# An attention and two-expert-layer kernel: the unit sizes of its last stage, the times its weights are split, and the order of its loads

## The chip, the cores and the metric

One core of a Trainium2 chip runs the whole kernel. The metric is the device time of one execution in microseconds (us); the kernel before takes 880.95 us, the median of three runs.

## What is computed

Attention over 4 batches and 8 heads of 64, with 32 global and 512 local rows each; a dense two-layer network on all 2176 rows; then a second network in which each row goes to one of eight experts. Only the last part is changed:

```python
logits = xn @ en.T / tau
expert_idx = np.argmax(logits, axis=1)
...
gate_w = probs[np.arange(N), expert_idx]
for e in range(E):                      # E = 8
    mask = expert_idx == e
    h = np.maximum(x[mask] @ w1[e], 0.0)        # w1[e]: 512 x 1024
    out[mask] = gate_w[mask, None] * (h @ w2[e])  # w2[e]: 1024 x 512
```

All data are float32. With the inputs of this case, the reference sends 153, 561, 160, 57, 46, 102, 1028 and 69 rows to the experts 0 to 7.

## The kernel before

**Stages.** Attention (slices 0 to 7 of the profile, roughly) runs beside the first steps of the dense network, whose rest (`L1`, `L2`, lines 678 to 712) follows; the logits and gates of finished rows are made along the way (`R0` to `R3`, for the last 384 rows `Q0` to `Q4`). The normal end of it is the expert stage, from about 618 us on. Rows with their gate lie in a table in memory, `x2d`; lists of row numbers, sorted by expert, lie in `idl`, padded so that each list may be read over its end. `make_plan` works out on DVE (on one partition) which list and which expert each unit gets, and leaves this in the tile `plan`.

**Units.** The expert stage is a fixed row of units, whatever the routing is. A unit fetches rows with an indirect DMA on the POOL queue (`gather`, line 857), transposes them on PE (`X2`, lines 929 to 952; 128x128 pieces against an identity), and runs both products. There are three kinds:

- Dense units of 256 rows (`D1`, line 1048, and `D2`, line 1066): for each of eight blocks of 128 hidden columns `D1` makes h transposed with twelve matmuls, ACT makes the relu of it (line 1054), DVE the rest that ACT's rounding leaves (line 1055), and `D2`, one step later, adds six matmuls to two output tiles. To keep float32's accuracy at the fast rate, weights and rows are held as a rounded part and a rest, and three of the four products are done.
- Units of 128 rows (`M1`, `M2`): the same with rows on the output's partitions, in two halves of 512 hidden columns each, and h transposed back by PE (`HT`, line 986).
- Mixed units of two rests of up to 64 rows of two experts (`X1`, line 974, and `X2M`, line 1033). Each half of PE's columns takes its own rows, and so the two experts' matmuls stand in pairs, in plain float32 on raw weights. A pass is `X1` or `X2M` for one half of the hidden columns; a unit has four passes.

The order is `ORDER` = 0, 1, 2, 3, S, 4, S, 5, 6, 7, mixed, mixed: eight dense units, two of 128 (S) and two mixed. Units 0 to 2 are planned before the last 384 rows are routed (phase 0 of `make_plan`), the others in three more phases that stand as pieces in units 0 to 3. What is over after all of this would be done by the code behind (`rest`, lines 1345 to 1366), under two branches on counts, which all engines read at the end.

**Weights.** One expert's weights are two matrices of 2.1 MB. `load_w` (lines 851 to 855) has SP read the expert from `plan` and issue the two loads, into lane a (`w1a`, `w2a`) or lane b (`w1b`, `w2b`). Where a unit has the expert of the one before it, the condition makes the load a no-op, but its weights are split again: `piece` (with `split`, lines 867 to 874) is a rounding copy on ACT (line 870) and a subtraction on DVE (line 871), over a quarter of a matrix. Each unit that isn't mixed has eight pieces, so 80 in all, written by the functions `some` and `ready` between the steps of the unit before. Split halves and lane b live in eight buffers called "half" (2.1 MB each).

**What sets the order.** In the expert stage DVE, ACT, SP and PE run in the order in which the code is written (`manual_schedule`). The function `unit` (lines 1278 to 1321) writes the steps, `due` (line 1323) hangs other work on a step, and `pend` holds second products back by a step.

## Time and profile before

| | |
|---|---|
| three runs, median (lowest to highest) | 880.95 us (880.47 to 881.92) |
| the profiled execution: its own time | 878.23 us |
| its span in the trace | 876.5 us |
| mean granted clock of PE | 0.973 |
| PE busy | 827.3 us, 94% |
| DVE, ACT, POOL busy | 502.8, 458.3, 159.8 us (57%, 52%, 18%) |
| moved by DMA | 91.73 MB, mean 105 GB/s |
| chain that ended last | PE 74%, DVE 7%, DMA 7%, issue 6%, ACT 5% |

The span is what the trace covers of the profiled execution, and all places in time are counted from its start. PE is a matmul, PEld the weight load of one, DVE, ACT and POOL the vector, scalar and general engine, SP the engine that issues most DMAs; a q behind a name is the engine's queue of instructions that aren't counted as busy. The granted clock is a share of 2.4 GHz. The trace leaves buffer and some tensor numbers out, and so `in_moe_w_dram` is either weight tensor of the experts. It shows every float32 matmul of a mixed unit as two records.

### The profile page before, as it was taken

The numbers are of one execution on the slowest core, as the hardware profiler recorded it, in microseconds if no ns is written. First come the engines' busy times: TensorE is split into PE (matmuls) and PEld (weight loads), VectorE is DVE, ScalarE is ACT, GpSimd is POOL, SyncE is SP. The second block draws the span as 40 slices with busy tenths as digits, with TensorE's granted clock in tenths as the row PEclk, the third lists the DMA queues.
The fourth block names the chain that finished last, engine by engine and source line by source line (L and its number), as shares of the span: only waits on it lengthen the run. The fifth ranks groups of instructions, "written<-read, shape, count | busy, mean of one in ns | idle before, by whom it ended". The sixth has DMA issues, their size and how long they took to land.

```text
span 876.5 us, 15818 instructions
## 1 busy us (share of the span) xinstructions
PE 827.3 (94%) x5764; PEld 694.3 (79%) x5764; DVE 502.8 (57%) x1369; ACT 458.3 (52%) x1143; POOL 159.8 (18%) x212
## 2 busy tenths in 40 slices
PE   6676698999999999999999999999999999999996
PEld 3554587888888888888888889889898988889841
DVE  6878989534654555365454442456678666766200
ACT  6877888444454545454453322325555566665221
POOL 3533354100120010010000000002113232421000
PEclk8787899999999999999999999999999999999998
DMA  8686555011012122011000000043042977716950
GB/s 237 179 214 164 149 165 144 20 40 37 25 43 48 30 59 46 13 47 33 2 13 13 1 25 1 13 151 103 25 37 78 380 257 250 244 69 236 365 211 19
DMA packets 103980, 91.73 MB, mean 105 GB/s; under 512 B 72967, under 2 KB 81287, under 8 KB 103890
## 3 DMA queue, kind: packets, MB, share of 16 engines
q1 hardware_dynamic: 97746, 78.51, 30.0%
q0 software_dynamic: 3744, 9.72, 3.3%
q10 hardware_dynamic: 2400, 2.36, 0.9%
q8 instruction: 49, 0.80, 0.5%
q14 instruction: 41, 0.34, 0.2%
HBM read 97.03 MB, written 11.10 MB: 123 GB/s over the span
## 4 chain that ended last, share of the span: by engine, by line
PE 74%; DVE 7%; DMA 7%; issue 6%; ACT 5%; SPq 0%; POOL 0%; ACTq 0%; POOLq 0%; DVEq 0%
PE hps L688 21%; PE hps L1048 8%; PE yp L710 7%; PE yp L1066 7%; PE yp L712 7%; PE yp L711 7%; DMA out_dram<-yo,ids 3%; PE av L256 2%; PE pp L242 2%; PE sp L205 2%; PE ga L317 2%; ACT pr L226 2%; DVE pr L232 1%; PE yp L1015 1%; PE hp L961 1%
## 5 line engine op out<-in xcount | busy, mean ns | idle before, releaser
L695 ACT COPY gf<-hps 128x256 f32<-128x256 f32 (+1 forms) x144 | 50.3, 361 | 173.9 <-PE hps L688 173.1
L696 DVE SCALAR_TENSOR_TENSOR gf<-gf 128x256 f32<-128x256 f32 (+1 forms) x144 | 60.0, 426 | 131.7 <-ACT gf L695 131.3
L710 PE MATMUL yp<-woh,g 128*128 128x512 f32 x272 | 114.2, 420 | 0.8 <-ACT g L698 0.8
L712 PE MATMUL yp<-woh,g 128*128 128x512 f32 x272 | 107.7, 396 | 1.5 <-DVE g L699 1.5
L711 PE MATMUL yp<-wol,g 128*128 128x512 f32 x272 | 107.4, 395 | 0.0
L1066 PE MATMUL yp<-w2s,g 128*128 128x512 f32 x384 | 101.0, 395 | 0.1
L699 DVE TENSOR_TENSOR g<-gf,g 128x256 fp32r<-128x256 f32 (+1 forms) x144 | 60.9, 431 | 42.8 <-ACT g L698 37.7
L1048 PE MATMUL hps<-xgT,w1s 128*128 128x256 f32 x512 | 82.6, 283 | 0.9 <-ACT xgT L947 0.9
L1066 PEld LDWEIGHTS yp<-w2s,g 128*128 128x128 f32 x384 | 67.5, 187 | 14.1 <-issue 1.6
L688 PE MATMUL hps<-xs,wih 128*128 128x256 f32 x448 | 75.6, 291 | 2.7 <-ACT gf L695 2.7
L1048 PEld LDWEIGHTS hps<-xgT,w1s 128*128 128x128 f32 x512 | 72.2, 188 | 5.6 <-ACT xgT L947 1.3
L698 ACT CAST g<-gf 128x256 fp32r<-128x256 f32 (+1 forms) x144 | 55.3, 395 | 35.0 <-DVE gf L696 34.9
L688 PEld LDWEIGHTS hps<-xs,wih 128*128 128x128 f32 x448 | 65.1, 189 | 9.3 <-ACT gf L695 3.1
L688 PE MATMUL hps<-xs,wil 128*128 128x256 f32 x448 | 71.2, 280 | 0.0
L688 PE MATMUL hps<-xl,wih 128*128 128x256 f32 x448 | 71.1, 280 | 0.0
L1054 ACT ACTIVATE g<-hps 128x256 fp32r<-128x256 f32 x64 | 24.6, 384 | 74.9 <-PE hps L1048 72.6
L712 PEld LDWEIGHTS yp<-woh,g 128*128 128x128 f32 x272 | 51.0, 188 | 14.6 <-DVE g L699 2.4
L710 PEld LDWEIGHTS yp<-woh,g 128*128 128x128 f32 x272 | 51.1, 188 | 12.8 <-issue 4.1
L688 PEld LDWEIGHTS hps<-xs,wil 128*128 128x128 f32 x448 | 60.9, 189 | 0.0
L688 PEld LDWEIGHTS hps<-xl,wih 128*128 128x128 f32 x448 | 60.9, 189 | 0.0
L711 PEld LDWEIGHTS yp<-wol,g 128*128 128x128 f32 x272 | 51.3, 188 | 6.5
L242 PE MATMUL pp<-ident,pr 128*128 128x128 f32 x256 | 41.7, 291 | 7.8 <-DVE pr L232 4.2
(285 smaller groups left out, 1625.2 us busy)
## 6 DMA issues: line engine op xcount, KB each, us to landing
w1a<-in_moe_w_dram SPq DMA_DIRECT2D x8, 2048.0 KB
w2a<-in_moe_w_dram SPq DMA_DIRECT2D x8, 2048.0 KB
w1b<-in_moe_w_dram SPq DMA_DIRECT2D x4, 2048.0 KB
w2b<-in_moe_w_dram SPq DMA_DIRECT2D x4, 2048.0 KB
wm<-in_moe_w_dram SPq DMA_DIRECT2D x4, 2048.0 KB
raw<-in_moe_w_in_dram SPq DMA_DIRECT2D x14, 512.0 KB
raw<-in_moe_w_out_dram SPq DMA_DIRECT2D x14, 512.0 KB
x2d<-x SPq DMA_DIRECT2D x16, 256.5 KB
```

The source lines that it names most:

```text
L242: nc.tensor.transpose(pp[:, j, :], pr[:, j // 2, (j % 2) * P:(j % 2) * P + P], ident)
L688: nc.tensor.matmul(hps, ws[a][:, k], xs[c][k], start=(a + c + k == 0), stop=((a, c) == (1, 0) and k == KM - 1))
L695: nc.scalar.copy(gf, hps[:, cs])
L696: nc.vector.scalar_tensor_tensor(out=gf, in0=gf, scalar=0.01, in1=gf, op0=ALU.mult, op1=ALU.max)
L698: nc.scalar.copy(g[:, 0], gf)
L699: nc.vector.tensor_tensor(out=g[:, 1], in0=gf, in1=g[:, 0].bitcast(F32), op=ALU.subtract)
L710: nc.tensor.matmul(yp, g[:, 0], hi, start=(f == 0), stop=False)
L711: nc.tensor.matmul(yp, g[:, 0], lo, start=False, stop=False)
L712: nc.tensor.matmul(yp, g[:, 1], hi, start=False, stop=(f == KF - 1))
L1048: nc.tensor.matmul(hps, w[:, a, k, fs], xts[u][c][:, k], start=(a + c + k == 0), stop=(a == 1 and k == KM - 1))
L1054: nc.scalar.activation(out=g[:, 0], in_=hps, func=AF.Relu)
L1066: nc.tensor.matmul(ys[u, t], g[:, a, t * P:(t + 1) * P], w[:, c, f % 4, :], start=(f + a + c == 0), stop=(f == KF2 - 1 and a == 1),)
```

## The change

The stage gets another row of units (`FIRST`): 0, 1, 2, S0, 3, QU, NE, NE + 1, S1, X0, S2, XL. There are six dense units, three of 128 rows (S0, S1, S2), two mixed ones of two halves (X0, XL) and a new one, QU, of four rests of up to 32 rows.

- Units 0 to 3 are all of the expert with most rows, NE and NE + 1 (4 and 5) of the second. Their weights are loaded and split once each (`weights_of`, `used_up`); with the three units of 128 that makes 5 × 8 = 40 pieces.
- `X1` and `X2M` take a list of two or four weights; with four, each matmul has 32 columns of its own (`tile_position`). The first products of QU stand ahead of NE, the second ones behind NE's last steps (`hold=True`).
- `early_plan` finds the two experts and `late_plan` makes all lists of 128, 64 and 32 in one pass (`lists`; a rest over 96 rows goes to a list of 128, one over 32 to a list of 64, others to a list of 32), in five pieces in units 0 and 1.
- Loads stand at fixed places, in `due`: `s_load` for a unit of 128, `f_load` for the second expert, `part_load` for the raw matrices of the rests; these go into "half" buffers or into lane a. QU has 16.8 MB of weights, X0 and XL have 8.39 MB each. Thirteen experts are loaded where there were ten.
- One branch on the count of unplaced lists (`more`) is left of two; the plan for what is over (`left_plan`) is made only inside it.

The core of the diff; the plan's own arithmetic is left out:

```diff
-    NDE, ND, NS, NM = 3, 8, 2, 2
-    NX = NBLK - 2 * (ND - NDE)
-    NENT, NCOL = ND + NX + E, 2 * ND + NX + E
-    HENT = ND + NX
+    QUART = P // 4
+    NE, NF, NS, NM = 4, 2, 3, 2
+    NEARLY = NE - 1
...
+    ND = NE + NF
+    SU, XU, QU, LU = ND, ND + NS, ND + NS + NM, ND + NS + NM + 1
...
+    SIZES = (P, HALF, QUART)
+    FEWEST = (96, 32, 0)
...
-    ORDER = [0, 1, 2, 3, ND, 4, ND + 1, 5, 6, 7, MIX, MIX + 1]
-    LANES = [[0, 1, 2, 3, 4, 5, 6, HENT], [ND, ND + 1, 7, HENT + 1]]
...
+    def weights_of(u):
+        return 0 if u < NE else NE if u < ND else u
...
+    def load_w(col, into, cond=False):
+        e = nc.sync.value_load(plan[0:1, 1, col:col + 1], min_val=0, max_val=E - 1)
+        cond = dict(cond=nc.sync.value_load(plan[0:1, 2, col:col + 1], min_val=0, max_val=1)) if cond else {}
+        for w, src in into:
             nc.sync.dma_start(w, src[bass.ds(e, 1)].rearrange("o (k p) f -> p (o k) f", p=P), **cond)
...
+    def to_split(w, pair, late_second):
+        sources[w] = pair
         order = [(1, 0), (1, 1), (2, 0), (2, 1)] if late_second else [(1, 0), (2, 0), (1, 1), (2, 1)]
-        return [(u, m, j, i) for m, j in order for i in range(2)]
-
-    for u in ORDER:
-        if u < MIX:
-            todo += new_pieces(u, u >= ND)
-
-    def loads():
-        for lane in range(2):
-            rest_ = [u for u in LANES[lane] if u not in loaded]
-            if not rest_ or phase_of(rest_[0]) > planned[0] or lane not in lanes:
-                continue
-            if any(lane_of[p[0]] == lane and p[0] in loaded for p in todo):
-                continue
-            load_w(rest_[0])
-            loaded.add(rest_[0])
+        todo.extend((w, m, j, i) for m, j in order for i in range(2))
...
+    def used_up(ws, u, j):
+        if u not in (0, 1, 2, NE):
+            ws.pop((weights_of(u), j))
+            freed()
...
-        w = w1s[u, j]
+        w = w1s[weights_of(u), j]
...
     def X1(u, j):
+        parts = raw[u]
+        n = P // len(parts)
         hp_ = ps.tile([P, DM], F32, tag="H", name="hp2")
         for k in range(KM):
-            for h in range(2):
-                r = slice(HALF * h, HALF * h + HALF)
+            for h, w in enumerate(parts):
+                r = slice(n * h, n * h + n)
                 nc.tensor.matmul(
-                    hp_[r], xts[u][0][:, k, r], raw[u][h][0][:, k, j * DM:(j + 1) * DM],
-                    start=(k == 0), stop=(k == KM - 1), tile_position=(0, HALF * h),
+                    hp_[r], xts[u][0][:, k, r], w[0][:, k, j * DM:(j + 1) * DM],
+                    start=(k == 0), stop=(k == KM - 1), tile_position=(0, n * h),
...
+    FIRST = [0, 1, 2, S0, 3, QU, NE, NE + 1, S1, X0, S2, XL]
...
+    def s_load(u, halves):
+        pair = [raw_half(m) for m in range(2)] if halves else lane
+        load_w(SC + u - SU, zip(pair, (w1, w2)), cond=True)
+        to_split(u, pair, True)
+
+    def f_load():
+        load_w(FC, zip(lane, (w1, w2)))
+        to_split(NE, lane, False)
+
+    def part_load(u, m, hs, to=None):
+        for i, h in enumerate(hs):
+            t = (w1_shape, w2_shape)[m](to[i]) if to else raw_half(m)
+            parts = raw.setdefault(u, [[None, None] for _ in range(2 if u < QU else 4)])
+            parts[h][m] = t
+            load_w((HC + 2 * (u - XU) if u < QU else QC) + h, [(t, (w1, w2)[m])])
...
+    def dense(u, first_behind):
+        x2 = next_rows(u)
+        for f in range(KF2):
+            D1(u, f)
+            behind(first_behind if f == 0 else len(pend))
+            hook(u, f)
+            if f in (5, 6):
+                x2(f - 5)
+            pend.append(lambda f=f: D2(u, f, 0))
+            pend.append(lambda f=f: D2(u, f, 1))
...
+    def block(u, hold=False):
+        first, second = (X1, X2M) if u >= XU else (M1, M2)
+        x2 = next_rows(u)
+        hook(u, 0)
         first(u, 0)
         behind()
+        hook(u, 1)
         x2(0)
         HT(u, 0)
-        some(1)
+        hook(u, 2)
         first(u, 1)
-        fetch()
+        fetch(u)
         behind()
+        hook(u, 3)
         x2(1)
         HT(u, 1)
-        some(1)
-        pend.extend([lambda j=j: second(u, j) for j in range(2)])
+        hook(u, 4)
+        if not hold:
+            pend.extend([lambda j=j: second(u, j) for j in range(2)])
...
+        (0, 0): [(Q1, 0), (Q1, 1), (Q0S, 0)],
+        (0, 1): [(Q1L, 0), (Q1L, 1), (Q1, 2), (Q0S, 1)],
+        (0, 2): [(Q1L, 2), (Q0S, 2)], (0, 3): [(Q2,)], (0, 4): [(Q3,)], (0, 5): [(Q4,)], (0, 6): [(plan_on,)],
+        (0, 7): [(plan_on,)],
+        (1, 0): [(plan_on,)], (1, 1): [(plan_on,)], (1, 2): [(s_load, S0, False), (plan_on,)],
+        (1, 3): [(load_ids, u) for u in (S0, 3, QU)] + [(load_ids, NE, 4)] + [(load_ids, u) for u in (S1, X0, S2, XL)],
+        (1, 6): [(fetch, 1)], (2, 1): [(some, 1), (fetch, 2)], (2, 7): [(some, 1), (f_load,)],
+        (S0, 3): [(part_load, QU, 0, (0, 1))],
+        (3, 1): [(fetch, 3), (part_load, QU, 0, (2, 3))],
+        (QU, 0): [(some, 1)], (QU, 3): [(freed, 4)], (QU, 4): [
+            (some, 2), (part_load, QU, 1, (2, 3)), (part_load, QU, 1, (0, 1), lane), (s_load, S1, True),
+        ],
+        (NE, 1): [(fetch, NE)], (NE + 1, 1): [(some, 1), (fetch, NE + 1)],
+        (NE + 1, 7): [(some, 1), (part_load, X0, 1, (0, 1))],
+        (S1, 1): [(s_load, S2, True)],
+        (X0, 1): [(some, 1)], (X0, 2): [(some, 1)],
+        (X0, 3): [(some, 1), (part_load, XL, 0, (0, 1), lane)], (X0, 4): [(some, 2)],
+        (S2, 0): [(some, 1)], (S2, 1): [(some, 1)], (S2, 2): [(some, 1)],
+        (S2, 3): [(freed, 2), (part_load, XL, 1, (0, 1))],
...
+    for f in (0, 2, 3, 4, 5, 6):
+        due.setdefault((2, f), []).append((some, 1))
+        due.setdefault((NE + 1, f), []).append((some, 1))
+    for f in (3, 4, 5, 6, 7):
+        due.setdefault((3, f), []).append((some, 1))
...
-        gather(ORDER[2])
-        for k in range(len(ORDER)):
-            if ORDER[k] == MIX:
-                raw[MIX] = lanes[0], lanes[1]
-            unit(k)
+        gather(FIRST[2])
+        for u in (0, 1, 2):
+            dense(u, 2)
+        block(S0)
+        dense(3, 1)
+        block(QU, hold=True)
+        dense(NE, 2)
+        X2M(QU, 0)
+        behind(2)
+        X2M(QU, 1)
+        freed(2)
+        part_load(X0, 0, (0, 1), lane)
+        dense(NE + 1, 2)
+        block(S1)
+        block(X0)
+        block(S2)
+        block(XL)
         behind(len(pend))
-    def rest(which, most, first, last, count=None):
-        if count is None:
-            count = nc.values_load(plan[0:1, 0, NCOL + which:NCOL + which + 1], min_val=0, max_val=most)
-        with tc.If(count > first):
-            for u in range((ND, HENT)[which] + first, (ND, HENT)[which] + first + 2):
-                ybank[u], lane_of[u] = "SY"[u % 2], u % 2
-                load_w(u)
-                loaded.add(u)
-                load_ids(u)
-                gather(u)
-                X2(u)
-                todo.extend(new_pieces(u, True))
-                for j in range(2):
-                    M1(u, j)
-                    HT(u, j)
-                for j in range(2):
-                    M2(u, j)
-            if first + 2 < last:
-                rest(which, most, first + 2, last, count)
-
-    rest(0, NX, NS, NX)
-    rest(1, E, 2 * NM, E)
+        assert not due and not todo, (due, todo)
+        freed(live[0])
...
+    def rest(first, count):
+        for u in range(LU + first, LU + first + 2):
+            ybank[u] = "SY"[u % 2]
+            pair = lane if u % 2 else [raw_half(m) for m in range(2)]
+            load_w(u - LU, zip(pair, (w1, w2)), cond=True)
...
+    more = nc.values_load(plan[0:1, 0, ZC:ZC + 1], min_val=0, max_val=NTILE + 3 * E)
+    with tc.If(more > 0):
+        left_plan()
+        rest(0, nc.values_load(plan[0:1, 0, NLEFT:NLEFT + 1], min_val=0, max_val=NLEFT))
```

How this moves instructions is seen in the order of the two built programs. First PE, at the first mixed unit of the kernel before (`hp` is the first product, `yp` the second, `tp` the transposed h):

```order
L1066 MATMUL yp_9723<-w2s,g_9885 128x512 x3
L986 MATMUL tp<-ident,hs 128x128 x4
L974 MATMUL hp_9955<-wm,xgT 64x512 x8
L1033 MATMUL yp_9966<-w2a,ht 64x512
L1033 MATMUL yp_9966<-w2b,ht 64x512
L1033 MATMUL yp_9966<-w2a,ht 64x512
```

Here two weights alternate in 64-column matmuls (`x8` counts equal rows on the second unit's `wm` buffers). In the changed kernel, PE at QU, between the last steps of unit 3 and NE's first:

```order
L1147 MATMUL yp_8308<-w2s,g_8460 128x512 x3
L1053 MATMUL hp_8498<-wm,xgT 32x512 x16
L1147 MATMUL yp_8304<-w2s,g_8484 128x512 x3
L1023 MATMUL xgp<-ident,xg 128x128 x4
L1065 MATMUL tp<-ident,hs 128x128 x4
L1053 MATMUL hp_8543<-wm,xgT 32x512 x16
L1147 MATMUL yp_8308<-w2s,g_8484 128x512 x3
L1023 MATMUL xgp<-ident,xg 128x128 x4
L1065 MATMUL tp<-ident,hs 128x128 x4
L1129 MATMUL hps_8663<-xgT,w1s 128x256 x4
```

QU's passes have 16 matmuls of 32 columns where a pass of a mixed unit has 8 of 64; its second products are not there, and NE's `D1` (line 1129) follows. They come where NE's last-but-one `D2` (line 1147) is done:

```order
L1129 MATMUL hps_8837<-xgT,w1s 128x256 x4
L1147 MATMUL yp_8695<-w2s,g_8819 128x512 x3
L1147 MATMUL yp_8699<-w2s,g_8819 128x512 x3
L1114 MATMUL yp_8859<-w1a,ht 32x512
L1114 MATMUL yp_8859<-w2a,ht 32x512
L1114 MATMUL yp_8859<-wm,ht 32x512 x2
```

So a whole dense unit stands between QU's first and second product. On ACT in unit 0, before (`g` is the relu of a step, `w1s` and `w2s` are pieces of the next unit's split weights):

```order
L1054 ACTIVATE g_7296<-hps_7283 128x256
L564 ACTIVATE sq,sl_7263<-x_7269 128x512
L870 CAST w1s<-w1a 128x1024
L1054 ACTIVATE g_7331<-hps_7318 128x256
L564 ACTIVATE sq,sl_7263<-x_7271 128x512
L870 CAST w1s<-w1a 128x1024
L1054 ACTIVATE g_7375<-hps_7362 128x256
```

and after:

```order
L1135 ACTIVATE g_7232<-hps_7219 128x256
L563 ACTIVATE sq,sl_7199<-x_7205 128x512
L1135 ACTIVATE g_7264<-hps_7251 128x256
L563 ACTIVATE sq,sl_7199<-x_7207 128x512
L1135 ACTIVATE g_7306<-hps_7293 128x256
L563 ACTIVATE sq,sl_7199<-x_7209 128x512
L1135 ACTIVATE g_7334<-hps_7321 128x256
```

The pieces that stood between unit 0's activations are gone from there; the relus and the activations of the last rows' logits stay.

## Rows read from the trace of the kernel before

**Rows 1.** The page, busy tenths and GB/s in 40 slices of 21.9 us
```profile
PE   6676698999999999999999999999999999999996
...
DMA  8686555011012122011000000043042977716950
GB/s 237 179 214 164 149 165 144 20 40 37 25 43 48 30 59 46 13 47 33 2 13 13 1 25 1 13 151 103 25 37 78 380 257 250 244 69 236 365 211 19
```

**Rows 2.** Windows: us, busy (x instructions) per engine, PEclk, DMA share, GB/s
```profile
618.20:645.20 27.00, 26.88 (x194) 24.25 (x193) 17.71 (x46) 14.27 (x27) 3.72 (x5) 1.00 0.36 49
668.55:691.88 23.33, 23.33 (x154) 21.03 (x154) 18.75 (x56) 13.02 (x20) 6.34 (x5) 1.00 0.74 268
714.76:751.56 36.80, 36.37 (x214) 31.38 (x213) 25.11 (x30) 23.83 (x35) 9.71 (x9) 1.00 0.78 274
835.10:867.30 32.20, 32.20 (x155) 11.91 (x154) 0.00 (x0) 6.96 (x12) 2.91 (x3) 1.00 0.32 118
```

**Rows 3.** Chain of waits, unit 0 and unit 3: start us, us, what
```profile
625.07 0.94 ACT w1s L870
...
626.36 0.83 issue
627.18 0.43 DVE g L1055
...
684.03 1.40 PE yp L1066 x6
685.43 0.44 PE xgp L946 x4
685.87 1.42 PE hps L1048 x12
```

**Rows 4.** PE timeline: start us, us, instruction [idle before it <- what ended it]
```profile
723.94 0.72 PE L1048 MATMUL hps<-xgT,w1s 128*128 128x256 f32 x4 [0.43 <-ACT xgT L947]
```

**Rows 5.** PE timeline, first pass of the first mixed unit
```profile
835.10 0.64 PE L974 MATMUL hp<-w1a,xgT 128*64 128x512 f32 x1
835.10 0.64 PE L974 MATMUL hp<-w1b,xgT 128*64 128x512 f32 x1
835.58 0.59 PE L974 MATMUL hp<-w1a,xgT 128*64 128x512 f32 x1
...
838.16 0.59 PE L974 MATMUL hp<-w1b,xgT 128*64 128x512 f32 x1
838.68 0.97 PE L1066 MATMUL yp<-w2s,g 128*128 128x512 f32 x3
```

**Rows 6.** PE timeline, attention of the global rows
```profile
237.17 1.08 PE L276 MATMUL sg<-kT,gz 64*32 64x512 f32 x8
238.05 0.26 PE L277 MATMUL sg<-kT,gz 64*32 64x32 f32 x8
```

**Rows 7.** Tile w1a: duration ns min/median/max, first and last start, shape
```profile
L870 ACT CAST w1s<-w1a x28: 1029/1042/1050, 593.9 to 782.2; 128x1024 fp32r<-128x1024 f32 x28
L871 DVE TENSOR_TENSOR w1s<-w1a,w1s x28: 1204/1218/1227, 594.9 to 783.5; 128x1024 fp32r<-128x1024 f32 x28
```

**Rows 8.** Lines 1347 and 1348, POOL's part, columns as above
```profile
L1347 POOLq TENSOR_LOAD <-plan x2: 303/402/501, 869.0 to 873.2; - x2
...
L1348 POOLq INC_SWDGE_SEM  x2: 317/332/348, 872.8 to 874.1; - x2
```

**Rows 9.** SP timeline, issues of loads into w1a at line 855
```profile
581.42 0.41 SPq L855 DMA_DIRECT2D w1a<-in_moe_w_dram  x1
...
643.84 0.09 SPq L855 DMA_DIRECT2D w1a<-in_moe_w_dram  x1
...
766.46 0.08 SPq L855 DMA_DIRECT2D w1a<-in_moe_w_dram  x1
```

**Rows 10.** Windows, two stretches of loads back to back, columns as above
```profile
680.00:700.00 20.00, 20.00 (x133) 18.02 (x132) 13.65 (x26) 11.42 (x18) 4.90 (x5) 1.00 1.02 387
820.00:840.00 20.00, 20.00 (x121) 15.46 (x120) 2.25 (x6) 3.37 (x8) 0.97 (x1) 1.00 1.03 402
```

More of the change, by code (lines that the diff above doesn't have):

```diff
@@ L740, in plan_constants @@
[L740 to L759 removed]
+        used[0] = 0
@@ new lines, in plan_constants, with before @@
+        c = late["c"] = dict(
+            edge=work(NJ), place=work(3, NLIST), size=work(3), ef=work(E), rf=work(E), full=work(NEARLY),
+            lt=work(E, E), done=work(E), cnt=work(E),
+        )
+        count_up(c["edge"], P)
+        count_up(c["ef"], 1)
+        count_up(c["rf"], -1, E)
+        count_up(c["full"], 2 * P, 2 * P)
+        for s in range(3):
+            count_up(c["place"][:, s], SIZES[s])
+            nc.gpsimd.memset(c["size"][:, s:s + 1], float(-SIZES[s]))
+    def before(lt, ef):
+        nc.vector.tensor_tensor(
+            out=lt, in0=ef.unsqueeze(1).to_broadcast([1, E, E]), in1=ef.unsqueeze(2).to_broadcast([1, E, E]), op=ALU.is_lt
+        )
@@ L842, in load_ids @@
[L842 to L854 removed]
+        shp = [1, 3, E, E]
@@ new lines, with cols_of, load_ids @@
+    xgs, xts, hss, hts, w1s, w2s = {}, {}, {}, {}, {}, {}
+    lane = []
+    def cols_of(u):
+        if u < ND:
+            return [2 * u, 2 * u + 1]
+        return [ND + u] if u < LU else [ND + LU + u % 2]
+    def weights_of(u):
+        return 0 if u < NE else NE if u < ND else u
+    def load_ids(u, tiles=None):
+        c = cols_of(u)[0]
+        if u < ND:
+            parts = [(c, slice(0, P), tiles or 2)]
+        elif u >= LU:
+            parts = [(u - LU, slice(0, P), 1)]
+        elif u < XU:
+            parts = [(SC + u - SU, slice(0, P), 1)]
+        else:
+            n = 2 if u < QU else 4
+            first = HC + 2 * (u - XU) if u < QU else QC
+            parts = [(first + h, slice(P // n * h, P // n * (h + 1)), 1) for h in range(n)]
+        for col, rows, m in parts:
+            o = nc.sync.value_load(plan[0:1, 0, col:col + 1], min_val=0, max_val=PADL if m < 3 else PADL - NT)
+            src = idl[bass.ds(o, m * (rows.stop - rows.start)), :]
+            nc.sync.dma_start(ids[rows, c:c + m], src.rearrange("(c p) o -> p (c o)", c=m) if m > 1 else src)
@@ L915, in piece @@
-            w, src = w2s[u, j], r2[:, 4 * j:4 * j + 4, :]
-        live[0] += i == 0
-        ins = split(w, src)[i]()
-        loads()
+                w2s[w, j] = half([P, 2, 4, DM], "w2s", F32R)
+            to, src = w2s[w, j], src[:, 4 * j:4 * j + 4, :]
+        ins = split(to, src)[i]()
+        if i == 1 and j == 1 and sources[w] is not lane:
+            freed()
         return ins
     def ready(u, m, j, last=1):
-        while any(p[:3] == (u, m, j) and p[3] <= last for p in todo):
-            assert piece() is not None, (u, m, j)
@@ L1192 @@
             plan_constants()
-            for _ in make_plan(0):
-                pass
-            loads()
-            for u in range(NDE):
+            early_plan()
+            load_w(0, zip(lane, (w1, w2)))
+            to_split(0, lane, False)
+            for u in range(NEARLY):
                 load_ids(u)
@@ L1276, in some, with hook, next_rows @@
             piece()
-    def unit(k):
-        u = ORDER[k]
-        ybank[u] = "SY"[k % 2]
-        after = ORDER[k + 1] if k + 1 < len(ORDER) else None
+    def hook(name, at):
+        for fn, *a in due.pop((name, at), []):
+            fn(*a)
+    def next_rows(u):
+        i = FIRST.index(u) + 1
+        after = FIRST[i] if i < len(FIRST) else None
         def x2(t):
@@ L1308, in unit, with fetch @@
-        first, second = (X1, X2M) if u >= MIX else (M1, M2)
-        some(2)
+        return x2
+    def fetch(u):
+        i = FIRST.index(u) + 2
+        if i < len(FIRST):
+            gather(FIRST[i])
+    def dense(u, first_behind):
[8 more added lines that the diff above has]
+            pend.append(lambda f=f: D2(u, f, 1))
@@ new lines @@
+        freed(live[0])
[4 more added lines that the diff above has]
+            load_w(u - LU, zip(pair, (w1, w2)), cond=True)
+            to_split(u, pair, True)
+            load_ids(u)
+            gather(u)
+            X2(u)
+            some(4)
+            for j in range(2):
+                M1(u, j)
+                HT(u, j)
+            some(4)
+            for j in range(2):
+                M2(u, j)
+        if first + 2 < NLEFT:
+            with tc.If(count > first + 2):
+                rest(first + 2, count)
```

375 lines of the change are left out of this document (185 added, 190 removed).

## Prediction

> **What bounds the kernel now.** First the page's busy shares in 40 slices [rows 1]: TensorE (PE) stands at nine tenths from slice 8 to the last but one, and the weights of the expert stage are loaded in slices 31 to 38, at up to 380 GB/s. PE's work ahead of that stage is the same in both kernels, so I cut the stage, 618.20 to 867.30 us, into units with the view by windows [rows 2]. A dense unit takes 23.33 us and PE is busy in all of it; the granted clock is 1.00 in every window, the upper of its two levels, 2.4 GHz; DVE and ACT are busy 18.75 and 13.02 us. So PE's own work sets the time, and a removed unit is worth its PE time as long as nobody else comes late. The chain of waits agrees [rows 3]: a dense unit is a row of steps of 1.42 us (line 1048) and 1.40 us (line 1066), with two transposes of gathered rows of 0.44 us.
>
> **What goes.** Eight dense units become six. Each is 8 × (1.42 + 1.40) + 2 × 0.44 = 23.4 us by the chain, 23.33 by the window, which I take: 2 × 23.33 = −46.66 us.
>
> **A third unit of 128 rows.** One such unit and the dense unit behind it take 36.80 us [rows 2]; less 23.33 that is 13.47. In it lies a wait of 0.43 us, of the dense unit for its transposed rows [rows 4]. Before, two dense units stand behind a small one; after, unit 3 stands behind the first small one and NE (the first unit of the second expert) behind QU (the unit of four rests), again two. So the added unit costs 13.47 − 0.43 = +13.04 us.
>
> **Four rests of 32 rows.** The two mixed units of two 64-row halves end the stage in 32.20 us [rows 2]. The last dense half step (1.40) is in that, and one transpose of gathered rows (0.44) lies ahead of it, so one mixed unit is (32.20 − 1.40 + 0.44) / 2 = 15.62 us. The timeline shows how [rows 5]: the two 64-column matmuls of a pair start together at 835.10, the next pair 0.48 later, the eighth and last at 838.16, the next work at 838.68. Seven steps in 3.06 us are 0.44 each, so a pass of eight pairs is some 3.43 to 3.58 us, and a mixed unit has four. QU has four passes too, with four 32-column matmuls in place of each pair. If four run at once, as two do now, the price is the same, +15.62. No 128-row matmul of 32 columns is in the trace. The nearest row is the attention's, 64 rows by 32 columns, also 512 long [rows 6]: eight start at 237.17 and the next group at 238.05, 0.88 / 8 = 0.11 us each, a quarter of 0.44. That is the rate of four at once, and I take 15.62. The other end is two at a time, a rival below.
>
> **Unit 0.** In the chain its third step waits until ACT has split a piece of the next unit's weights (0.94), then 0.83 and 0.43 until DVE has made its part of g [rows 3]. Much of that lies beside logit matmuls: the window has 27.00 us, PE 26.88, which is 3.6 over a dense unit [rows 2]. Now no split stands between unit 0's activations. I take −0.9, about the piece itself, with 0 and −1.8 (0.94 + 0.83) as ends.
>
> **NE's first step.** Two pieces of the second expert's split now stand behind QU, ahead of NE's first g: 2 × 1.04 us on ACT, 2 × 1.22 on DVE [rows 7]. Behind the waiting g stands NE's first product with the second matrix, as in unit 0 today. So +0.9, the same jam; at least 0, at most 2 × 1.22 = 2.4.
>
> **The other splits** are 40 pieces in place of 80. Each took 1.04 and 1.22 us beside a PE that was busy all the time [rows 2, 7], so their end gives nothing: 0. The early plan has fewer DVE steps, under a PE of nine tenths: 0. The late plan's steps stand on DVE in units 0 and 1, in place of the pieces that are gone: 0. If that cover is too thin, g is late next, a jam of the kind priced above.
>
> **The tail.** Behind the last output, POOL reads and passes two leftover branches: counts at 869.0 and 873.2, last semaphore steps at 872.8 and 874.1 [rows 8]. One is left: 872.8 − 874.1 = −1.3 us, between 0 (the output is awaited anyway) and −2.6.
>
> **The loads.** Of SP's issues, a load whose condition is false takes 0.07 to 0.09 us, a real one 0.41 [rows 9]: 643.84 is one of three pairs of repeats of the first expert, 766.46 of one of another. Ten experts' weights of 4.19 MB are loaded before, thirteen after. The first critical set is QU's second matrices, 8.39 MB, which may start when QU's first product has read its own. PE then does a half step (0.70), two transposes (0.44 each), the wait of 0.43, the 0.9 above and NE's steps (8 × 1.42, 7 × 1.40, 2 × 0.44): 24.9 us. While loads run back to back the DMA moves 387 and 402 GB/s [rows 10]. The first load was issued at 581.42 [rows 9] and its first piece split at 593.9 [rows 7], 12.5 us for 4.19 MB, which are 10.4 at 402: about 2.1 us of start. So QU's set takes 2.1 + 20.9 = 23.0 us, at 387 23.8, in time by 1.9 or 1.1; it decides at 8.39 / 22.8 = 368 GB/s. The last unit's first matrices (4.19 MB, 12.5 us) have three steps of a 128 unit (2.9 each: 13.04 less three transposes, by four), two mixed passes and four transposes ahead of them, some 17 us; its second ones two steps, two passes and three transposes, 14 us. All in time: 0.
> The Trainium skill ("DMA: Bandwidth & Descriptors", Specifications) speaks against that: it gives about 358 GB/s as the memory's limit for one core. By that figure QU's set would come 25.5 − 24.9 = 0.6 us late and the gain below would shrink by 0.6; the trace's 402 GB/s over 20 us lies above it, and the measurement decides.
>
> **Sum.** −46.66 + 13.04 + 15.62 − 0.9 + 0.9 − 1.3 = −19.3 us on the span of 876.5: 857.2. The profiled execution took 878.23 us itself, 2.72 below the median of the runs, 880.95. So 858.9 for such an execution, **861.6** as the median. With all low ends (−1.8, 0, −2.6) 858.5; with all high ones (0, +2.4, 0) and a pass of 3.58 for 3.43 in QU (+0.6), 866.
>
> **Rivals.**
> 1. Only two of the 32-column matmuls run at once. Each of QU's four passes takes 3.43 us more: +13.7, 875.3. For it: at 128 rows only pairs are seen [rows 5]. Against: [rows 6].
> 2. Loads come a little late, because buffers come free later than I reckon or the rate is lower. At 340 GB/s QU's set is 24.7 + 2.1 − 24.9 = 1.9 us late; 2 to 10 us in all give 864 to 872. For it: margins of 1 to 2 us. Against: [rows 10].
> 3. Slower: loads become the bound. QU's first product is done at 618.20 + 26.1 + 2 × 23.33 + 36.80 + 8.4 = 736.2 us (the 8.4: two passes, a half step, two transposes). From 738.3, after the start, 33.55 MB must come until the last unit's second product: QU's 8.39, then 4.19, 8.39, 4.19, 8.39. In slices 33 to 35 the rate is 257, 250 and 244 GB/s [rows 1]. At 244 it takes 137.5 us, to 875.8; with two passes (6.9) and 7.9 of tail (876.5 − 867.3 − 1.3) the span is 890.6, 14.1 more than before: 895.0. It is slower than before under 33.55 / (876.5 − 14.8 − 738.3) = 272 GB/s. Against: in those slices loads were waited for by nobody and asked for with pauses; [rows 10] is the rate without.
> 4. The change doesn't do what it says: rows don't fit the lists and leftover units run, two at a time. One is a load of 12.5 us, eight pieces of 1.22 and 13 us of PE, 35 us; two partly side by side give 35 to 70 more, 897 to 932. Against: the reference's routing gives the experts 153, 561, 160, 57, 46, 102, 1028 and 69 rows. 1028 and 561 fill the dense units, with 4 and 49 over; 128, 128 and 102 are the small units; 49, 57, 46 and 64 the halves; 25, 32, 4 and 5 the quarters. Nothing is left, but no list is free either, and the 32 just fit.
>
> **How the numbers follow.** The forecast has 0.74: a row backs each of its two open points, four at once and the rate. Rival 1 has 0.09, rival 2 0.08, rival 3 0.04, rival 4 0.03; 0.02 is for what I don't see. The range, 857 to 876, goes from the low sum less the runs' scatter (1.4 us) to rival 1 and holds rival 2; the forecast alone would have 858 to 867. A measurement tells 0.2%, 1.8 us, from no change. Faster is the forecast with rivals 1 and most of 2: 0.89; within 0.2%: 0.02; slower, rivals 3 and 4 and the unseen: 0.09.
>
> **What would show it.** Right: QU's four passes of 3.4 to 3.6 us (6.9: rival 1); PE busy through NE and no load awaited ahead of QU's second product; unit 0 near 26.1 us; one wait ended by DVE at NE's start; 40 pieces; one branch in the tail; PE's end near 849. Wrong: PE idle for over 3 us after 736 and a DMA that ends it (rivals 2, 3), leftover units (4), or dense steps that are no longer 1.42 and 1.40.

## The result, and the profile after

The changed kernel takes 866.12 us, the median of four runs (863.86 to 868.36), where the kernel before takes 880.96: a ratio of 0.983 with a 95% interval of 0.980 to 0.986. So it is faster, by 14.8 us where 19.3 were forecast. The profiled execution took 863.86 us itself, its span is 862.1, 14.4 under the span before and 4.9 over the 857.2 of the sum.

The page after, in 40 slices, answers to [rows 1]:

```profile
PE   6766698999999999999999999999999999999996
...
DMA  9785555112012212111100000016136697798890
GB/s 228 181 217 161 144 157 170 27 38 47 13 45 44 46 31 56 33 26 39 19 2 26 1 13 13 14 16 220 47 37 114 174 383 296 274 390 326 326 391 29
```

PE is as full as before. The loads now run at 274 to 391 GB/s in slices 32 to 38, counted from 0 as the prediction's 31 to 38 are (its 33 to 35 are counted from 1), without the hole of 69 that [rows 1] has.

I cut the expert stage where the units begin: unit 0's first product, S0's, QU's, S1's, and the last unit's second product. The view by windows (us, busy time of PE, PEld, DVE, ACT and POOL, granted clock, DMA share, GB/s) answers to [rows 2]:

```profile
619.31:692.09 72.78, 72.78 (x492) 65.91 (x491) 33.05 (x104) 24.92 (x50) 16.23 (x20) 1.00 0.55 114
692.09:729.02 36.93, 36.50 (x214) 31.22 (x212) 12.10 (x17) 13.63 (x25) 6.71 (x9) 1.00 0.96 375
729.02:796.53 67.51, 64.87 (x445) 47.31 (x445) 23.10 (x32) 24.64 (x42) 10.26 (x14) 1.00 0.85 314
796.53:848.08 51.55, 51.50 (x243) 29.77 (x241) 14.13 (x14) 20.70 (x32) 3.89 (x4) 1.00 0.82 305
848.08:862.10 14.02, 7.09 (x33) 2.21 (x32) 0.00 (x0) 1.57 (x3) 1.94 (x2) 0.86 0.10 36
```

The sum, put into the same stretches, had 72.76 (26.1 + 2 × 23.33), 36.80, 63.61 (15.62 + 2 × 23.33 + 0.43 + 0.9), and 51.9 us for the fourth (two units of 128, two mixed ones and the 1.40, less the last two passes). Three of these are met within 0.4 us. The third, from QU to S1, is 67.51, 3.9 us too long, and PE is idle there for 2.6. The stage also begins 1.1 us later than before, 619.31 for 618.20, with the same work ahead of it.

What PE waited for in the stage, from the view of waits (us in total, times, longest):

```profile
PE yp L1114 <- DMA w2a<-in_moe_w_dram: 1.9, 1, 1.9
PE hps L1129 <- ACT xgT L1024: 0.9, 2, 0.4
PE yp L1147 <- DVE g L1136: 0.3, 1, 0.3
```

The waits for `xgT` and for g were expected: two of 0.43 us, and one of 0.35 in place of the 0.9 that was taken. The wait for a load ahead of QU's second product was not. The PE timeline at QU's first product and at its second, which answers to [rows 5] and [rows 6]:

```profile
729.02 3.64 PE L1053 MATMUL hp<-wm,xgT 128*32 128x512 f32 x32
732.59 0.96 PE L1147 MATMUL yp<-w2s,g 128*128 128x512 f32 x3
...
734.35 3.64 PE L1053 MATMUL hp<-wm,xgT 128*32 128x512 f32 x32
```

```profile
763.23 1.04 PE L1114 MATMUL yp<-w1a,ht 128*32 128x512 f32 x2
766.14 0.62 PE L1114 MATMUL yp<-w2a,ht 128*32 128x512 f32 x1 [1.86 <-DMA w2a<-in_moe_w_dram]
...
769.70 1.67 PE L1147 MATMUL yp<-w2s,g 128*128 128x512 f32 x6
```

Four 32-column matmuls do run at once: 32 of them take 3.57 us (729.02 to 732.59), as a pass of pairs does. At the second product two matmuls start at 763.23, on weights that are there, and the next ones only at 766.14. From 763.23 to the dense step at 769.70 that pass takes 6.47 us, 2.9 more than a pass of the first product.

The tail: one branch of POOL's, with one count and one last semaphore step, answers to [rows 8].

```profile
L1486 POOLq TENSOR_LOAD <-plan x1: 504/504/504, 856.1 to 856.1; - x1
```

```profile
L1487 POOLq INC_SWDGE_SEM  x1: 408/408/408, 859.9 to 859.9; - x1
```

From the last unit's second product to the end it is 14.02 us where it was 876.5 − 860.69 = 15.8 before.

### The profile page after: what moved, and what is told of

Its sections match the earlier page's. It is cut to its first block, busy times and chain, and to the rows that moved or that the text cites. A ratio compares the mean times of both kernels' runs of the same rounds, so it can differ in the third digit from the quotient of the medians.

```text
span 862.1 us, 15349 instructions
## 1 busy us (share of the span) xinstructions
PE 813.5 (94%) x5660; PEld 669.1 (78%) x5660; DVE 443.5 (51%) x1266; ACT 417.1 (48%) x1091; POOL 143.7 (17%) x210
## 4 chain that ended last, share of the span: by engine, by line
PE 73%; issue 8%; DMA 7%; DVE 6%; ACT 5%; POOL 0%; POOLq 0%; ACTq 0%; DVEq 0%
PE hps L687 22%; PE yp L709 8%; PE yp L711 7%; PE yp L710 7%; PE hps L1129 6%; PE yp L1147 6%; DMA out_dram<-yo,ids 4%; PE sp L204 3%; PE pp L241 3%; PE av L255 3%; ACT pr L225 2%; PE ga L316 1%; DMA raw<-in_moe_w_in_dram 1%; DVE pr L231 1%; PE lp L506 1%
## 5 line engine op out<-in xcount | busy, mean ns | idle before, releaser
L1147 PE MATMUL yp<-w2s,g 128*128 128x512 f32 x288 | 76.1, 396 | 0.3 <-DVE g L1136 0.3
L1129 PE MATMUL hps<-xgT,w1s 128*128 128x256 f32 x384 | 61.9, 283 | 0.9 <-ACT xgT L1024 0.9
L1147 PEld LDWEIGHTS yp<-w2s,g 128*128 128x128 f32 x288 | 50.6, 187 | 12.2 <-issue 2.5
L1136 DVE SCALAR_TENSOR_TENSOR g<-hps,g 128x256 fp32r<-128x256 f32 x48 | 20.3, 424 | 73.9 <-ACT g L1135 73.9
L1129 PEld LDWEIGHTS hps<-xgT,w1s 128*128 128x128 f32 x384 | 53.8, 188 | 5.0 <-ACT xgT L1024 1.3
L1135 ACT ACTIVATE g<-hps 128x256 fp32r<-128x256 f32 x48 | 18.5, 384 | 73.8 <-PE hps L1129 73.7
```

The costliest lines, as they stand in the source:

```text
L1129: nc.tensor.matmul(hps, w[:, a, k, fs], xts[u][c][:, k], start=(a + c + k == 0), stop=(a == 1 and k == KM - 1))
L1147: nc.tensor.matmul(ys[u, t], g[:, a, t * P:(t + 1) * P], w[:, c, f % 4, :], start=(f + a + c == 0), stop=(f == KF2 - 1 and a == 1),)
```

## The experiments

Twelve runs on three chips: a0, e1, e2 and e3 on one, f1, f2, f3 and e4b on a second, g2, g3, a1 and f3b on a third, each time with the kernel before beside them. f2, g2 and g3, which leave out something that the result needs, ran once each. "Units 0 to 2" and "QU to S1" are the first and third stretch above, of each run's profile.

| run | median us | ratio to before | units 0 to 2 | QU to S1 |
|---|---|---|---|---|
| changed, first profile | 866.12 | 0.983 (0.980 to 0.986) | 72.78 | 67.51 |
| a0, changed again | 872.71 | 0.990 (0.987 to 0.994) | 75.55 | 67.93 |
| e1, S1's load later | 871.91 | 0.988 (0.985 to 0.992) | 78.00 | 67.49 |
| e2, half of QU's set | 867.28 | 0.983 (0.980 to 0.986) | 76.73 | 64.61 |
| e3, QU's second later | 867.08 | 0.985 (0.981 to 0.988) | 78.75 | 64.28 |
| f1, S0's pieces later | 866.21 | 0.985 (0.983 to 0.987) | 72.78 | 67.46 |
| f2, no late scatter | 864.21, one | | 72.78 | 66.79 |
| f3, both moves | 863.28 | 0.982 (0.980 to 0.984) | 72.78 | 64.32 |
| e4b, f3 and a second split | 863.28 | 0.981 (0.979 to 0.983) | 73.19 | 64.29 |
| g2, no load for S1 | 867.46, one | | 74.63 | 67.69 |
| g3, no outputs of unit 3 | 869.11, one | | 76.87 | 66.62 |
| a1, changed, third time | 870.17 | 0.986 (0.982 to 0.990) | 75.83 | 69.49 |
| f3b, both moves again | 865.97 | 0.981 (0.978 to 0.985) | 76.42 | 64.42 |

The kernel before has medians of 881.63, 880.64 and 881.69 us on the three chips (11 runs each).

**a0, the changed kernel again.** No edit.

> The changed kernel once more, beside the three below on one chip. Its first four runs lie between 863.9 and 868.4 us, the kernel before's between 880.5 and 881.9. Theory (the spread comes from the late load of QU's second matrices): the profile shows PE waiting 2 to 6 us for that load, more in a slow run than in a fast one. Rival (the spread comes from ahead of the expert stage): the wait stays near the 2.9 us of the first profile and the stage starts earlier or later than at 619.3.

On this chip it takes 872.71 us. The wait at QU is the same, so the first theory falls: the spread is not from there. The rival, that it comes from ahead of the stage, holds for 2.4 us of the 5.9 by which the span is longer: the stage begins at 621.74. More of it lies in units 0 to 2, which take 75.55 us in place of 72.78. A wait that the first profile doesn't have stands in unit 2. It costs most in e3's profile, on the same chip; first ACT, then PE (start us, us, instruction, in brackets the idle time before it and what ended it):

```profile
677.71 1.04 ACT L957 CAST w1s<-w1a 128x1024 fp32r<-128x1024 f32 x1 [4.57 <-DMA w1a<-in_moe_w_dram]
678.66 0.38 ACT L1135 ACTIVATE g<-hps 128x256 fp32r<-128x256 f32 x1
```

```profile
675.96 0.63 PE L1129 MATMUL hps<-xgT,w1s 128*128 128x256 f32 x4
679.09 3.38 PE L1147 MATMUL yp<-w2s,g 128*128 128x512 f32 x6 [2.50 <-ACT g L1135]
682.27 1.05 PE L1129 MATMUL hps<-xgT,w1s 128*128 128x256 f32 x4
```

ACT stands ready at 673.1 with the first split piece of S0, and S0's matrix lands 4.57 us later. Unit 2's relu stands behind that piece on ACT, and PE needs it: idle for 2.50 us. Then PE is slow as well: four 256-column matmuls from 682.27 to the next group take 0.85 us, not 0.47. The windows show the granted clock (third column from the end):

```profile
676.00:678.00 2.00, 0.59 (x6) 0.38 (x4) 0.00 (x0) 0.29 (x1) 0.25 (x1) 1.00 0.70 193
680.00:682.00 2.00, 1.91 (x5) 1.31 (x5) 2.00 (x5) 1.19 (x2) 0.00 (x0) 0.50 1.01 352
682.00:684.00 2.00, 2.00 (x11) 1.90 (x10) 0.94 (x1) 0.00 (x0) 0.00 (x0) 0.50 0.30 79
686.00:688.00 2.00, 2.00 (x16) 1.86 (x15) 1.22 (x1) 0.39 (x1) 1.51 (x2) 1.00 0.49 134
```

It is 0.50, the lower level of 1.2 GHz, from 680 to 684, behind a stretch (676 to 678) in which PE was busy for 0.59 of 2.00 us, and 1.00 again at 686. Both together cost 78.75 − 72.78 = 6.0 us. In the first profile the same matrix came 0.36 us after ACT was ready for it, and nothing was lost.

**e1, S1's load later.** The `s_load` of S1 is moved from behind QU's loads to the end of NE:

```diff
-            (some, 2), (part_load, QU, 1, (2, 3)), (part_load, QU, 1, (0, 1), lane), (s_load, S1, True),
+            (some, 2), (part_load, QU, 1, (2, 3)), (part_load, QU, 1, (0, 1), lane),
...
-        (NE, 1): [(fetch, NE)], (NE + 1, 1): [(some, 1), (fetch, NE + 1)],
+        (NE, 1): [(fetch, NE)], (NE, 7): [(s_load, S1, True)], (NE + 1, 1): [(some, 1), (fetch, NE + 1)],
```

> The load of unit S1's weights (4.19 MB) is issued at the end of NE, no longer right behind QU's second set. Theory A (loads issued later take a share of the DMA engines from those before them): 10.1 MB move between 738 and 766 us where QU's set is 8.39 MB; without S1's share the set lands up to 4 us earlier, PE's wait of 2.9 us before QU's second product goes, the time falls by 2 to 3 us. Theory B (loads are served in the order of issue, and the rest of the bytes are gathers and outputs): wait and time stay as they are, 2.9 us and some 866.

Inconclusive by its own fault: SP had nothing to wait for between the two places, and issued S1's load 14.2 us after QU's first one (756.11 and 741.96), as before the move (751.87 and 738.02, 13.9). The place in the code of an issue is no time. g2 below asks the question again.

**e2, half of QU's set.** `part_load` issues no load for the two matrices that go into lane a.

> Two of QU's four second matrices aren't loaded (those of lane a; QU's second product runs on what lies there, so its rows of two experts aren't computed from their own weights). Theory (that load is what ends late): 4.19 MB less in the way, no wait of PE before QU's second product, span down by 2.9 us to about 859, and the spread over the runs falls to about that of the kernel before, 1.5 us. Rival (PE would be held there anyway, or the spread has another source): span 861 to 862 as now, or runs still 4 us apart.

QU to S1 is 64.61 us in place of 67.5 to 67.9, with no wait for a load: 2.9 to 3.3 us are that load's. The runs lie closer together, 865.7 to 868.5, than a0's, 869.8 to 874.4, but the wait in unit 2 is there still (76.73), so the median can't be read as the first theory wanted.

**e3, QU's second product one dense step later.**

```diff
         dense(NE, 2)
-        X2M(QU, 0)
-        behind(2)
-        X2M(QU, 1)
-        freed(2)
-        part_load(X0, 0, (0, 1), lane)
         dense(NE + 1, 2)
...
+        (NE + 1, 0): [(X2M, QU, 0), (X2M, QU, 1), (freed, 2), (part_load, X0, 0, (0, 1), lane)],
```

> QU's second product, both passes together, stands one dense step (1.42 and 1.40 us) later: behind the first step of NE + 1 and the last one of NE. Theory (only this load is late, everything behind has slack): the wait of 2.9 us shrinks to nearly 0, time down by 2.5 to 3 us. Rival (the loads as a whole are the limit from there on): X0's first matrices, which take the place of QU's, start later by 3 to 4 us, and the time saved comes back as a wait for X0, S2 or XL: no gain.

QU to S1 takes 64.28 us, 3.2 less than in the first profile, and no later unit waits for a load. The median is 867.08 us against a0's 872.71, though its profile shows the costliest jam in unit 2 of all. The theory stands: only this set is late here, the loads behind have slack.

**f1, S0's pieces three steps later.** The eight pieces of S0 stand in steps 3 to 7 of unit 2.

```diff
-        (1, 6): [(fetch, 1)], (2, 1): [(some, 1), (fetch, 2)], (2, 7): [(some, 1), (f_load,)],
+        (1, 6): [(fetch, 1)], (2, 1): [(fetch, 2)], (2, 7): [(some, 2), (f_load,)],
...
+    for f, n in ((3, 1), (4, 2), (5, 1), (6, 2)):
+        due.setdefault((2, f), []).append((some, n))
```

> The eight split pieces of unit S0 stand in steps 3 to 7 of unit 2 (1, 2, 1, 2, 2) in place of steps 0 to 7, three steps or 8.4 us later; nothing else is moved. Theory (S0's load, issued at 653, lands only at 673 to 679 us, ACT waits for it with the relus of unit 2 behind the piece, PE idles 2 to 3 us and then runs some 5 us at a granted clock of 0.50): that wait and the stretch of low clock go, units 0 to 2 take 72.8 to 73.5 us as in the first profile of the changed kernel, where the same four runs on this chip took 75.6 to 78.8; the time falls by 3 to 6 us against the 872.7 us of the repeated kernel. Rival (the clock falls for another reason, and the wait follows from it): a stretch at 0.50 stays in unit 2, no gain.

Units 0 to 2 take 72.78 us, to the hundredth what they take in the first profile, with no wait in them and no low clock. The median is 866.21, on a chip where the changed kernel itself was not run; against a0 on another it is 6.5 less. That isn't shown to be the move's. On this chip the load comes earlier: in e4b's profile it lands 20.3 us after its issue, at 675.8. In the first profile ACT comes to the first piece 53.6 us after the stage's start; in e4b's, whose stage starts at 621.15, that would be at 674.7, so it would have waited about 1.1 us (an estimate). In g2's profile ACT waits 2.8 us and units 0 to 2 lose 1.9. There was hardly a loss to remove; f3b below is the better test of the move.

**f2, no scatter of the last rows' numbers.** In the changed kernel S0's load is issued at 652.98, and the first piece of it is split at 673.24, 20 us for a matrix of 2.1 MB, which are some 5 us at 402 GB/s. Between 639.90 and the landing of the load POOL's queue issues three scatters, each behind the end of the one before (POOL timeline), and the windows show what the DMA engines do (last two columns: their busy share, GB/s):

```profile
639.90 1.07 POOL L640 DMA_INDIRECT idl<-tok,si  x1 [9.66 <-DVE sl L634]
651.02 0.97 POOL L640 DMA_INDIRECT idl<-tok,si  x1 [10.06 <-DMA idl<-tok,si]
659.62 0.96 POOL L640 DMA_INDIRECT idl<-tok,si  x1 [7.63 <-DMA idl<-tok,si]
```

```profile
655.00:658.00 3.00, 3.00 (x22) 2.72 (x21) 0.80 (x4) 0.38 (x1) 0.00 (x0) 1.00 0.46 25
658.00:661.00 3.00, 3.00 (x22) 2.72 (x22) 0.42 (x1) 0.38 (x1) 1.08 (x2) 1.00 0.40 49
```

They are busy for 0.40 to 0.46 of the time and move 25 to 49 GB/s. This busy time isn't the scatters'. The view of DMA from 655 to 661 puts it down to SP's queue, which is the load, with 54 packets:

```profile
q1 hardware_dynamic: 54, 0.22, 43.0%
```

And in the kernel before, which has the same scatters at that time and no load beside them (650.58 and 657.80 are its second and third), the engines show next to nothing:

```profile
650.00:654.00 4.00, 4.00 (x27) 3.58 (x26) 3.83 (x13) 2.27 (x4) 1.25 (x1) 1.00 0.01 0
654.00:658.00 4.00, 4.00 (x29) 3.68 (x29) 3.70 (x18) 1.42 (x3) 0.20 (x1) 1.00 0.04 2
```

f2 leaves the three scatters out:

```diff
-            nc.gpsimd.indirect_dma_start(
-                out=idl[:, :], out_offset=bass.IndirectOffsetOnAxis(ap=si[:, q:q + 1], axis=0),
-                in_=tok[:, t:t + 1], in_offset=None,
-            )
```

> The three scatters that write the last 384 rows' numbers into the lists are left out (those rows are then in no list and are not computed; the counts, the plan and the loads stay). Theory (these scatters hold the DMA engines with little moved, 0 to 50 GB/s between 643 and 661, and S0's load waits behind them): S0's first matrix, issued near 653, lands within 8 us, by 661, and ACT doesn't wait for it. Rival (a load with a condition, or the one behind it, is slow by itself): it lands as late as now, 20 us or more after its issue.

The same windows of f2, and ACT at the first piece:

```profile
655.00:658.00 3.00, 3.00 (x21) 2.67 (x20) 1.77 (x9) 0.38 (x1) 0.12 (x1) 1.00 0.80 243
658.00:661.00 3.00, 3.00 (x21) 2.67 (x20) 0.42 (x1) 0.38 (x1) 0.00 (x0) 1.00 1.00 407
```

```profile
673.92 1.04 ACT L953 CAST w1s<-w1a 128x1024 fp32r<-128x1024 f32 x1
```

The load issued at 654.11 moves at 243, then 407 GB/s (SP's queue has 1.69 MB from 655 to 661, where it had 0.22), and the piece at 673.92 waits for nothing. So the scatters held it, not its condition. A scatter writes 128 numbers of 4 bytes to 128 places, and in the first profile the three take 10.5, 8.3 and 12.6 us from issue to landing. The Trainium skill ("DMA: Bandwidth & Descriptors", Specifications) says that transfers under 512 B don't run at line rate, because the DMA engine reads, modifies and writes. The trace agrees in that 512 bytes take that long; why they hold up another queue's load no run here shows. f2's stretch at QU isn't compared, since its lists lack 384 numbers.

**f3, both moves.**

> Both moves together: S0's pieces three steps later, QU's second product one dense step later. Theory (two waits for loads, each hidden by a move): no wait of PE for a load, none of over 0.5 us at all in the expert stage, span near 859 and 861 to 863 us as the median; the spread over runs falls to about 2 us. Rival (each move gives back elsewhere): X0, S2 or XL wait for their loads, 865 or more.

The median is 863.28 us, 2.9 under f1's on the same chip; the profiled run took 859.76 with a span of 858.0. What PE waits for in its expert stage is this and nothing else:

```profile
PE hps L1129 <- ACT xgT L1024: 0.9, 2, 0.4
PE yp L1147 <- DVE g L1136: 0.3, 1, 0.3
```

Five runs still lie between 859.8 and 865.7 us, wider than the 2 us expected.

**e4b, splitting once undone for one unit.** On top of f3, units 1 to 3 use a second set of split halves, made in unit 0.

```diff
-        return 0 if u < NE else NE if u < ND else u
+        return 0 if u < 1 else 1 if u < NE else NE if u < ND else u
...
+    to_split(1, lane, False)
...
+    for f in range(KF2):
+        due.setdefault((0, f), []).append((some, 1))
```

> As the one before, but the first expert's weights are split a second time for unit 1, eight pieces of 1.04 us on ACT and 1.22 on DVE in unit 0, as the kernel before has them. Theory (splits lie beside PE, only unit 0's are partly seen): unit 0 0.3 to 0.9 us longer, nothing else, time up by under 1 us. Rival (splitting once is where the gain comes from): 2 us or more for these eight of the 40 pieces that were saved.

The same median, 863.28, and units 0 to 2 take 73.19 us, 0.41 more, all of it in unit 0 (26.85 us for 26.44). The chain of waits in unit 0 is that of [rows 3] again:

```profile
628.03 0.95 ACT w1s L957
...
629.31 0.83 issue
630.14 0.43 DVE g L1136
```

**g2, no load for S1.** S1 runs on the second expert's split weights; its `s_load` and pieces go.

> S1 has no load and no split of its own (it runs on the second expert's split weights, so its rows are not computed with their own): what e1 was to do and didn't, since SP issued the load at the same place in time there. Theory A (a load issued later takes a share from those before it): PE's wait before QU's second product falls from 2.9 us to under 1. Theory B (loads are served in the order of issue; QU's set shares the engines with gathers and outputs alone, some 1.6 MB): the wait stays within 0.4 us of 2.9.

PE waits 1.94 us for QU's load where it waited 1.86, and QU to S1 is 67.69 us. Theory B: S1's load costs QU's nothing.

**g3, no outputs of unit 3.** `out_rows` returns before its DMA for unit 3.

> Unit 3's two output DMAs are left out (256 rows aren't written). Theory B (six indirect DMAs of 0.26 MB each, four gathers and these two outputs, go ahead of QU's last weights): 0.52 MB less at 390 GB/s is 1.3 us, the wait falls from 2.9 to about 1.6 us. Rival (only weight loads count, the rest goes beside them): 2.9 us as now.

The wait for the load falls from 1.9 to 1.0 us and QU to S1 to 66.62, 0.9 less than in the first profile. On its own chip it is 1.1 less than in g2. Theory B had 1.3; the rival had 0. Only the two outputs were tried in this way, not the four fetches.

**a1 and f3b, on one chip.** No further edit.

> The changed kernel beside the next one on one chip. Theory: 866 to 873 us, by whether S0's load holds PE up in unit 2 (0 to 6 us, with the clock at 0.50 behind it where it idles long), and 2.9 us at QU in every run.

> Both moves again (S0's pieces three steps, QU's second product one dense step later), beside the changed kernel on the same chip. Theory: 860 to 865 us, 3 to 9 us under the changed kernel of the same call; no wait of PE for a load. Rival (the chip made the difference): within 2 us of it.

They take 870.17 and 865.97 us: 4.2 less with both moves, inside the 3 to 9 expected, and 1 us over the 865. a1's profile has 2.0 us of waiting for QU's second set and 0.8 for its first one, which is why QU to S1 is longest there. But f3b's profile has a wait in unit 2, which the theory had not:

```profile
690.46 0.63 PE L1023 MATMUL xgp<-ident,xg 128*128 128x128 f32 x4 [1.92 <-DMA xg<-x2d,ids]
...
691.64 1.05 PE L1129 MATMUL hps<-xgl,w1s 128*128 128x256 f32 x4
```

This is the fetch of S0's rows. It needs the row numbers, and these need the scatters, which on this chip ended later: 690.46 is PE's start after 1.92 us of waiting for the rows, and the four matmuls at 691.64 take twice their time again. The move of the pieces does what it should on ACT: the load lands 23.8 us after its issue, at 679.1, and the first piece at 681.83 waits for nothing, where a1's waits 4.0 us. But PE is then held by the rows, and units 0 to 2 take 76.42 us for a1's 75.83. So the gain on this chip is QU's, 64.42 for 69.49. The two moves take away what waits for the weights, not what waits for the lists.

## Why the prediction was right or wrong

**Right: what bounds the stage.** Less work on PE is less time, term for term. Where no load is late the stretches come out near the sum: units 0 to 2 at 72.78 (72.76 forecast) in all four profiles without a wait there, S0 and unit 3 at 36.93 (36.80), the four last units at 51.55 (51.9), QU to S1 at 64.32 in f3 (63.61). The total is 866.12 for the 861.6 of the forecast, 4.5 us too long, and the way there was rival 2's, which had 0.08. Rival 1 is out: four at once, 3.57 us a pass, the upper end of the 3.43 to 3.58. Rivals 3 and 4 are out too: no run is slower than before, and no leftover unit runs.

**Splits: 0 was right, unit 0's −0.9 was too much.** From its first product to unit 1's, unit 0 takes 26.84 us before, 26.44 after, and 26.85 in e4b, which puts its eight pieces back: the change gave 0.4. That units 0 to 2 meet the forecast to 0.02 us is luck: unit 0 is 0.3 over its 26.1, and unit 2, the last one ahead of a small unit, takes 22.95 and not 23.33, as unit 3 does before (22.89).

**NE's first step** costs 0.35, not 0.9. **The tail** gave 1.5 to 2.0 (13.8 to 14.3 us in the profiles), not 1.3.

**Wrong: "All in time: 0."** This is the term that failed, at two places.

The first is QU's set, the step "so QU's set takes 2.1 + 20.9 = 23.0 us". PE was ready after 25 us, as reckoned: 738.02 SP's first issue, 763.23 the second product. But the set needed 28.1. The rate from 750 on was near the lower of the two reckoned with, 387 GB/s; the view by windows has it, and SP's timeline has the issues:

```profile
738.02 1.60 SPq L942 DMA_DIRECT2D wm<-in_moe_w_dram  x2
740.45 3.84 SPq L942 DMA_DIRECT2D w1a<-in_moe_w_dram  x1
745.11 5.24 SPq L942 DMA_DIRECT2D w2a<-in_moe_w_dram  x1
751.87 6.98 SPq L942 DMA_DIRECT2D wm<-in_moe_w_dram  x2
```

```profile
740.00:750.00 10.00, 9.46 (x62) 8.34 (x63) 4.14 (x6) 3.76 (x8) 2.49 (x3) 1.00 1.00 358
750.00:760.00 10.00, 10.00 (x65) 8.86 (x64) 2.39 (x5) 1.95 (x5) 1.05 (x1) 1.00 1.05 388
764.00:766.00 2.00, 0.28 (x1) 0.00 (x0) 0.00 (x0) 0.00 (x0) 0.00 (x0) 1.00 1.04 408
```

What I left out is that the weights aren't alone. Between 734 and 762 POOL issues six indirect DMAs of 0.26 MB, four fetches of rows and two outputs:

```profile
734.78 1.00 POOL L947 DMA_INDIRECT xg<-x2d,ids  x1 [9.49 <-issue]
736.09 1.02 POOL L1081 DMA_INDIRECT out_dram<-yo,ids  x1 [0.31 <-issue]
...
740.08 1.05 POOL L947 DMA_INDIRECT xg<-x2d,ids  x1 [2.77 <-issue]
741.43 1.02 POOL L1081 DMA_INDIRECT out_dram<-yo,ids  x1 [0.30 <-issue]
...
758.26 1.05 POOL L947 DMA_INDIRECT xg<-x2d,ids  x1 [15.39 <-issue]
761.25 1.00 POOL L947 DMA_INDIRECT xg<-x2d,ids  x1 [1.94 <-issue]
```

They are 1.6 MB, of which the view of DMA has 1.05 between 738.02 and 766.14: 2.7 us at 390 GB/s, which makes 25.7 of the 28.1 us. The other 2.4 are slower stretches, such as 358 GB/s from 740 to 750; what slowed them no run shows. g2 and g3 agree: the load behind takes nothing from QU's, and the two outputs take 0.9 to 1.1 us. The 2.1 us of start were a misreading besides: the first piece at 593.9 starts without a wait behind other work of ACT's, and needs one of the two matrices; the view of DMA has 3.99 of the 4.19 MB moved by 594, so the start is nearer 2.6 us. Rival 2 is what happened, at 2.9 to 3.2 us, with a cause that I hadn't named. By the estimate from the 358 GB/s of the Trainium skill ("DMA: Bandwidth & Descriptors", Specifications) the set would have been 0.6 us late. It was 2.9 late with 388 GB/s from 750 to 760 and 408 at the end, so that figure isn't the reason, though all that moved in the 28.1 us, slow stretches and all, comes to a mean of 360.

The second is S0's load, which no term of the sum has. Before, the loads of that time are no-ops [rows 9], so the trace of before couldn't show one waiting; the scatters were there to be seen. It costs 0 in the first profile and 1.9 to 6.0 us in the seven other profiles of kernels that keep the scatters, and the pieces where the change has them (a0, e1, e2, e3, g2, g3, a1). f2 shows the scatters' part; e3's timelines show the piece that stands first in line on ACT, and f3b that it waits no more three steps later. How late the load is goes with the last scatter: that takes 12.3 to 12.8 us to land in the first profile, f1, f3 and e4b, and 13.3 to 14.2 in e1, g2, g3, a1 and f3b. In the five profiles that record both, the load lands 1.6 to 2.3 us behind it. The medians of 870.17 and 872.71 on other chips, 4 to 7 us over the first, go with it: a0's and a1's profiles have 2.8 and 3.1 us there.

**Of the 4.9 us** between 857.2 and 862.1, 3.9 are the stretch from QU to S1 (3.2 the load, by f3's 64.32; by 0.7 the stretch is too long without it), 1.1 the later start of the stage, 0.2 the two stretches ahead of QU; the last units and the tail took 1.0 back (51.55 for 51.9, 14.02 for 14.76). The 0.8 that is left is how the cut by stretches differs from the sum. The start lies between 618.0 and 622.2 us in the profiles of kernels that are alike ahead of it; what moves it was not tried.

**Open:** why the scatters take longer on some chips than on the first. The spread that is left in f3 (6 us) fits the start of the stage and the fetch of f3b, but only two profiles stand behind that.

## What to carry to other kernels

Reckon a load's time with everything that moves beside it, also the fetches and outputs of units that are done: add their bytes, then divide. Where a load becomes real work for the first time, look at what other queues have under way there, also where the DMA engines' busy share is near 0, as it is during the scatters of single numbers in the kernel before. Put nothing that waits for such a load in front of an activation that PE needs. A second product that waits for weights can be moved behind the next step of another unit, if what takes its buffers has slack: here that is 3 us.
